# Two score buffers, two job banks: both outputs of a job share one two-bank score buffer, the freed bank becomes a seventh score bank, and single banks are released by split exponentials

## The chip, the cores and the metric

The kernel runs on one core of a Trainium2 chip. The metric is the device time of one execution in microseconds (us). The engines are named as the profile names them: PE (matmul), PEld (the weight loads that run ahead of the matmuls), DVE, ACT, POOL, and SP, which only issues transfers.

## The reference

One block of 2048 tokens with 512 features: 32 attention heads of width 16 that share one key and one value head, a gated feed-forward layer with 1376 inner features, and a per-token gate that mixes the two.

```python
g = sigmoid((x * gate_w).sum(-1, keepdims=True))
q = (x @ wq) -> 32 heads of 16;  k = x @ wk;  v = x @ wv
p = softmax(q @ k.T * 16 ** -0.5)           # per head, 2048 x 2048
a = (p @ v -> 2048 x 512) @ wo
b = (gelu_tanh(x @ w_gate) * (x @ w_up)) @ w_down
return g * a + (1 - g) * b                  # all in fp32; wq and wk are drawn 8 times larger
```

## The kernel before

After a prologue (projections of q, k, v, the first feed-forward chunk) everything is one long list of steps for PE, written out by hand as `PLAN`, 62 lines. `play` reads a line letter by letter, and PE executes the instructions in that order. The kinds of work are:

- **S (a score pair).** `scores(n, third)` makes the scores of two heads for 128 keys and 512 queries: two matmuls of 51 rows (L745), one on rows 0 to 63 and one on rows 64 to 127 of the array, which write the two banks of one score buffer of 2 x 512 fp32. Then ACT takes the exponential of all 1024 columns in one instruction (L749) into a buffer `p`. There are 1024 such pairs. `S` uses score buffers 0 and 1 in turn, `Z` uses buffer 2.
- **V (a value visit).** `pv` multiplies the exponentials of two score pairs (four heads) with the values: four products on four column strips of 32 (L816; the profile shows two matmul instructions for each, so eight for a V). They are summed over 16 V in the one bank `acc`. After the 16th, `norm` has DVE copy `acc` out (L759 or L770), and the next V needs that bank. There are 512 V.
- **F (one step of a job).** A job is a pair of long matmul chains into two banks z and y: gate and up projection of a feed-forward chunk (`gate_job`, 24 F), a part of the down projection (`down_job`), or the output projection (`wo_job`). `H` takes the banks and makes the generator `pair_mm`; each `F` issues one z matmul and one y matmul (L515), on the two row halves; `R` ends the job and has its banks evacuated. There are 61 jobs with 1608 F.
- **T** lets the GELU chain of the last gate job go on to its Tanh on ACT; the rest of the chain (`outer`, `halves`) follows two and three score pairs later.

`pair_mm` runs each chain in two halves. In the first half z is computed on the lower rows and y on the upper, in the second half the other way round. So in the middle of a job each bank passes from one row half to the other, and a no-operation on POOL (`relay`, L523) waits for the last matmuls of the first half; the first matmuls of the second half wait for it. At every third F `slot` issues a queued piece of DVE and POOL work: splitting a weight tile in two parts (`split_part`: DVE cast L186, POOL subtraction L187, then `fetch` issues the next load on SP), or a step of the softmax normalisation (`bg`).

The PSUM pools are three score buffers of two banks each (`ps_s`), one bank for `acc` (`ps_a`) and one bank (`ps_f`). While a job runs, z lies in the first bank of score buffer 2 and y in the `ps_f` bank, so that two score buffers are left; the second bank of buffer 2 lies idle. At `R` a gate job's `gelu` copies z to SBUF (L541), and runs `inner` (L544, L545); y stays in its bank until `outer` (L552), behind the Tanh.

Weight tiles arrive from DRAM in a ring of four staging buffers `st`, three loads ahead. The order on each engine is fixed when the kernel is built; at run time the engines only wait for one another.

Of the kernel before, what the change touches and what calls it, by code (L numbers as in the profile page):

```python
# [19 lines left out]
P = 128  # L20
S = 2048
# [22 lines left out]
STAGE = 4  # L44
PLAN = [
# [66 lines left out]
def mix_kernel(ctx, tc, xT, wq, wo, wf, out):  # L112
# [424 lines left out]
    def gelu(n, g, u):  # L537
        flush(chain)
        gs = cp.tile([P, TG], F32, tag="gs", name=f"gs{n}", bufs=1)
        sq = cp.tile([P, TG], F32, tag="sq", name=f"sq{n}", bufs=1)  # L540
        nc.vector.tensor_copy(gs, g)  # L541

        def inner():
            nc.vector.scalar_tensor_tensor(sq, gs, GC, gs, op0=ALU.mult, op1=ALU.mult)  # L544
            nc.vector.scalar_tensor_tensor(sq, sq, 1.0, gs, op0=ALU.add, op1=ALU.mult)  # L545

        def tanh():
            nc.scalar.activation(sq, sq, AF.Tanh, bias=0.0, scale=GS)  # L548

        def outer():  # L550
            nc.vector.scalar_tensor_tensor(sq, sq, 1.0, gs, op0=ALU.add, op1=ALU.mult)
            nc.vector.scalar_tensor_tensor(gs, u(), 0.5, sq, op0=ALU.mult, op1=ALU.mult)  # L552

        def halves():
            hh, hl = h_tiles(n)
            nc.vector.tensor_copy(hh, gs)
            nc.vector.tensor_sub(hl, gs, hh)
            hold.append((n, hh, hl))

        chain.extend((inner, tanh, outer, halves))  # L560
# [14 lines left out]
    def gate_job(n):  # L575
        tg, r = chunks[n]

        def begin():
            flush(todo)
            queue_parts(parts(n))  # L580
            return weights_terms(n, 0), weights_terms(n, 1)

        def end(z, y):
            gelu(n, z, lambda: y)
            advance(3)()
            if r == NF - 1 and tg + 1 < NTG:
                queue_parts(x_parts(tg + 1))

        return begin, end
# [134 lines left out]
    gelu(1, g1, lambda: up1)  # L724
# [4 lines left out]
    at = {}  # L729

    def scores(n, third):
# [10 lines left out]
        ps = two_banks("s", 2 if third else next(i for i in turn if i < 2))  # L742
        for j in range(2):
            rs = slice(64 * j, 64 * j + QK)
            nc.tensor.matmul(ps[:, j * TG : (j + 1) * TG], kp[rs, kc * P : (kc + 1) * P],  # L745
                             Q[u][rs, pr], start=True, stop=True)
        if pr == 0:
            pb[s] = m2.tile([P, 2, 2 * TG], F32, tag="p", name="p", bufs=PB // 2)
        nc.scalar.activation(pb[s][:, pr], ps, AF.Exp, bias=0.0, scale=SCALE)  # L749
# [72 lines left out]
    def score(third):  # L822
        scores(at_s[0], third)
# [11 lines left out]
    def play(word, job):  # L835
        if job:
            X, Y = job[0]()
        for t in word.split():
            k = int(t[1:] or 1)
            if t[0] in "SZ":  # L840
                for _ in range(k):
                    score(t[0] == "Z")
# [89 lines left out]
```

## Time and profile before

| | |
|---|---|
| median of 3 runs | 1230.35 us (1230.30 to 1230.39) |
| span of the profiled execution | 1229.5 us, mean granted clock 0.999 |
| prologue, 0 to 80.5 us | PE busy 78.29 us |
| list of steps, 80.5 to 1213.8 us | PE busy 1133.17 us, ACT busy 993.55 us, DVE 473.65 us |
| last output projection, 1213.8 to 1229.5 us | PE busy 11.12 us |
| exponentials | 1024 of 1024 columns, 976.3 us on ACT |
| score pairs / V / F in the list | 1024 / 512 / 1608 |

The profiled execution's own time is known by its span, 0.85 us under the median of the runs. Matmuls are pipelined and their ends modelled, so that PE's busy share says little; what counts is the spacing of their starts. A row of the timeline gives start, duration, engine, line, operation, output from inputs, and in brackets how long the engine stood idle before it and what the profile takes for the releaser.

### The profile page before, as it was taken

The page shows a single profiled execution, that of the slowest core. Times are in us where ns is not written, and L with a number is a line of the kernel's source. Part 1 is how long each engine was busy: PE and PEld are TensorE (multiplying, and loading weights), DVE is VectorE, ACT ScalarE, POOL GpSimd, SP SyncE. Part 2 cuts the span into 40 slices and gives each one's busy share as a digit, 9 for nine tenths or more (in the row PEclk, how much of TensorE's full clock was granted, in tenths as well). Part 3 has the DMA queues.
Part 4 walks back from the last instruction along what each step waited for, and adds up shares of the span by engine and source line. Part 5 has one row for each costly group of instructions (what it writes and reads, how often), then busy time and mean ns, then how long its engine had stood idle before and what let it go on. Part 6 is the DMA issues. An engine that isn't in the chain of part 4 may idle for free.

```text
span 1229.5 us, 23232 instructions
## 1 busy us (share of the span) xinstructions
PE 1222.6 (99%) x9742; PEld 671.4 (55%) x9742; DVE 546.1 (44%) x812; ACT 1029.4 (84%) x1127; POOL 216.9 (18%) x188
## 2 busy tenths in 40 slices
PE   9999999999999999999999999999999999999998
PEld 6875455555554555455555555654554555545545
DVE  7774422656245151545436152263626244044624
ACT  5549888888888888998888888889888898889983
POOL 5422201222121010212112020121311011012100
PEclk9999999999999999999999999999999999999999
DMA  8641202212021110122211120111211211002000
GB/s 333 211 135 52 72 1 58 66 53 79 27 68 51 44 32 23 49 57 67 66 35 58 39 76 15 42 44 56 83 41 49 75 49 32 23 27 66 15 1 35
DMA packets 39835, 73.88 MB, mean 60 GB/s; under 512 B 5488, under 2 KB 5744, under 8 KB 39728
## 3 DMA queue, kind: packets, MB, share of 16 engines
q1 hardware_dynamic: 39184, 71.32, 18.9%
q8 instruction: 77, 1.26, 0.4%
q0 software_dynamic: 256, 0.79, 0.2%
q14 instruction: 30, 0.25, 0.1%
q10 hardware_dynamic: 288, 0.26, 0.1%
HBM read 57.41 MB, written 14.94 MB: 59 GB/s over the span
## 4 chain that ended last, share of the span: by engine, by line
PE 93%; DVE 0%; ACT 0%; issue 0%
PE acc L816 38%; PE s L745 23%; PE z L515 21%; PE y L515 10%; PE wos L501 1%; PE u L501 0%; DVE acc L627 0%; ACT p L749 0%; PE wof L501 0%; DVE sq L545 0%; DVE sq L544 0%; DVE gs L541 0%; ACT sq L548 0%
## 5 line engine op out<-in xcount | busy, mean ns | idle before, releaser
L749 ACT ACTIVATE p<-s 128x1024 f32<-128x1024 f32 x1024 | 976.3, 1026 | 139.1 <-PE s L745 136.2
L816 PE MATMUL acc<-p,v 128*32 128x512 f32 x4096 | 484.8, 597 | 0.0
L745 PE MATMUL s<-Q,kp 51*128 51x512 f32 x2048 | 384.8, 415 | 0.1
L745 PEld LDWEIGHTS s<-Q,kp 51*128 51x128 f32 x2048 | 184.2, 184 | 214.1 <-ACT p L749 124.0
L816 PEld LDWEIGHTS acc<-p,v 128*32 128x32 f32 x4096 | 114.3, 109 | 250.8 <-issue 242.1
L187 POOL TENSOR_TENSOR gl<-st,gh 128x512 fp32r<-128x512 f32 x80 | 114.0, 1444 | 754.3 <-PE s L745 375.5
L515 PE MATMUL z<-xh,gh 64*128 64x512 f32 x312 | 125.9, 403 | 0.0
L515 PE MATMUL y<-xh,gh 64*128 64x512 f32 x312 | 125.8, 403 | 0.0
L515 PE MATMUL y<-xl,gh 64*128 64x512 f32 x312 | 122.4, 392 | 0.0
L515 PE MATMUL z<-xl,gh 64*128 64x512 f32 x312 | 122.1, 391 | 0.0
L515 PE MATMUL z<-xh,gl 64*128 64x512 f32 x312 | 121.8, 390 | 0.0
L515 PE MATMUL y<-xh,gl 64*128 64x512 f32 x312 | 121.7, 390 | 0.0
L541 DVE COPY gs<-z 128x512 f32<-128x512 f32 x39 | 27.0, 692 | 195.3 <-PE y L515 128.5
L187 POOL TENSOR_TENSOR dl<-st,dh 128x512 fp32r<-128x512 f32 x44 | 57.3, 1304 | 127.8 <-PE s L745 94.0
L515 PE MATMUL z<-dh,hh 64*128 64x512 f32 x176 | 69.5, 395 | 0.0
L515 PE MATMUL y<-dh,hh 64*128 64x512 f32 x176 | 69.5, 395 | 0.0
L515 PE MATMUL y<-dl,hh 64*128 64x512 f32 x176 | 68.9, 392 | 0.0
L515 PE MATMUL z<-dl,hh 64*128 64x512 f32 x176 | 68.8, 391 | 0.0
L515 PE MATMUL z<-dh,hl 64*128 64x512 f32 x176 | 68.8, 391 | 0.0
L515 PE MATMUL y<-dh,hl 64*128 64x512 f32 x176 | 68.7, 391 | 0.0
L515 PEld LDWEIGHTS z<-xh,gh 64*128 64x128 f32 x312 | 58.0, 186 | 15.6 <-POOLq L523 7.3
L515 PEld LDWEIGHTS z<-xl,gh 64*128 64x128 f32 x312 | 58.3, 187 | 8.2
(173 smaller groups left out, 1458.0 us busy)
## 6 DMA issues: line engine op xcount, KB each, us to landing
st<-wf SPq DMA_DIRECT2D x125, 256.0 KB
scr<-q SPq DMA_DIRECT2D x16, 512.0 KB
Q<-scr SPq DMA_DIRECT2D x64, 128.0 KB
Q<-scr SPq DMA_DIRECT2D x64, 64.0 KB
out<-acc SPq DMA_DIRECT2D x16, 256.0 KB
xr<-xT SPq DMA_DIRECT2D x6, 512.0 KB
st<-xT SPq DMA_DIRECT2D x12, 256.0 KB
xr<-xT SPq DMA_DIRECT2D x4, 256.0 KB
```

What stands on the lines that cost most here:

```text
L187: eng_l.tensor_sub(lo, src, hi)
L501: nc.tensor.matmul(ps, a, b, start=(first and q == 0), stop=(last and q == len(terms) - 1), skip_group_check=True)
L515: mm = nc.tensor.matmul(ps, a[rs], b[rs], start=(half == 0 and q == 0), stop=(half == 1 and q == len(X) - 1), skip_group_check=True)
L541: nc.vector.tensor_copy(gs, g)
L745: nc.tensor.matmul(ps[:, j * TG : (j + 1) * TG], kp[rs, kc * P : (kc + 1) * P], Q[u][rs, pr], start=True, stop=True)
L749: nc.scalar.activation(pb[s][:, pr], ps, AF.Exp, bias=0.0, scale=SCALE)
L816: nc.tensor.matmul(accp[u][32 * j : 32 * j + 32], vt[:, kc], pb[s][:, j // 2, (j % 2) * TG : (j % 2 + 1) * TG], start=(kc == 0), stop=(kc ...
```

## The change

- z and y are now the two banks of score buffer 2 (`z, y = bank[4:6]`). At `R` a gate job's `gelu` copies z to `gs` and at once forms `t = 0.5 * y * gs` from y; the chain then needs no PSUM: `inner` works from `gs`, its scratch tile `sq` comes from the staging ring `st`, and `outer` is one product with `t`. The number of DVE instructions is the same (seven for a chunk).
- The `ps_f` bank is a seventh score bank, `bank[6]`, for the whole list. The score buffers are allocated once, and the dependencies go by the bank written or read.
- A step for scores now names its banks: `A`, `B`, `C` are the three buffers with one exponential of 1024 columns; `a`, `b`, `c` are the same buffers with two exponentials of 512 columns; a digit `i` puts the first head in bank 6 and the second in bank `i`, with two exponentials of 512.
- The list of steps is new. It has the same 1024 score pairs, 512 V, 61 jobs and 1608 F. 448 of the score pairs have one exponential, 576 have two (283 small letters, 293 digits).

The diff, cut to its core (three of the 62 lines of the list):

```diff
+SCORES = "ABCabc012345"
 PLAN = [
-    "t: S2",
-    "f: H F7 S F3 S F2 S F3 S F3 S F3 S F3 R S V Z S T S V3 S Z S V2 S",
-    "f: H F3 S F3 S F4 S F2 S V S F3 S F3 S F3 S F3 R S V S2 T Z V3 S2 Z V3 S Z S V2 S",
-    "f: H F3 S F3 S F3 S F3 S F3 S F3 S F3 S F3 R S V S2 T Z V3 S2 Z V3 Z S2 V2 S",
...
+    "t:",
+    "f: H F 0 F4 B F3 1 F4 B 0 F6 B F3 a F3 R B 0 V4 T B",
+    "f: H F2 A F3 B F3 a F4 b 0 F5 B F5 1 F2 R b V2 A T C 2 V3 A 3",
+    "f: H F5 A F4 b F3 a 2 V2 A F2 B F4 a F3 2 F3 R A 3 V2 A T 2 c V3 A B",
...
     def gelu(n, g, u):
         flush(chain)
         gs = cp.tile([P, TG], F32, tag="gs", name=f"gs{n}", bufs=1)
-        sq = cp.tile([P, TG], F32, tag="sq", name=f"sq{n}", bufs=1)
+        t = cp.tile([P, TG], F32, tag="sq", name=f"t{n}", bufs=1)
         nc.vector.tensor_copy(gs, g)
+        nc.vector.scalar_tensor_tensor(t, u, 0.5, gs, op0=ALU.mult, op1=ALU.mult)
 
         def inner():
+            sq = cp.tile([P, TG], F32, tag="st", name="sq", bufs=STAGE)
             nc.vector.scalar_tensor_tensor(sq, gs, GC, gs, op0=ALU.mult, op1=ALU.mult)
-            nc.vector.scalar_tensor_tensor(sq, sq, 1.0, gs, op0=ALU.add, op1=ALU.mult)
+            nc.vector.scalar_tensor_tensor(gs, sq, 1.0, gs, op0=ALU.add, op1=ALU.mult)
 
         def tanh():
-            nc.scalar.activation(sq, sq, AF.Tanh, bias=0.0, scale=GS)
+            nc.scalar.activation(gs, gs, AF.Tanh, bias=0.0, scale=GS)
 
         def outer():
-            nc.vector.scalar_tensor_tensor(sq, sq, 1.0, gs, op0=ALU.add, op1=ALU.mult)
-            nc.vector.scalar_tensor_tensor(gs, u(), 0.5, sq, op0=ALU.mult, op1=ALU.mult)
+            nc.vector.scalar_tensor_tensor(t, gs, 1.0, t, op0=ALU.add, op1=ALU.mult)
...
+    pair = [ps_s.tile([P, 2 * TG], F32, tag=f"s{i}", name=f"pair{i}") for i in range(3)]
+    bank = [pair[i // 2][:, i % 2 * TG : i % 2 * TG + TG] for i in range(6)]
+    bank.append(ps_f.tile([P, TG], F32, tag="pf", name="bank6"))
 
-    def scores(n, third):
+    def scores(n, where):
...
-        ps = two_banks("s", 2 if third else next(i for i in turn if i < 2))
+        if where.isdigit():
+            two = 6, int(where)
+        else:
+            i = "abc".index(where.lower())
+            two = 2 * i, 2 * i + 1
         for j in range(2):
             rs = slice(64 * j, 64 * j + QK)
-            nc.tensor.matmul(ps[:, j * TG : (j + 1) * TG], kp[rs, kc * P : (kc + 1) * P],
-                             Q[u][rs, pr], start=True, stop=True)
+            nc.tensor.matmul(bank[two[j]], kp[rs, kc * P : (kc + 1) * P], Q[u][rs, pr], start=True, stop=True)
...
-        nc.scalar.activation(pb[s][:, pr], ps, AF.Exp, bias=0.0, scale=SCALE)
+        if where.isupper():
+            nc.scalar.activation(pb[s][:, pr], pair[i], AF.Exp, bias=0.0, scale=SCALE)
+        else:
+            for j in range(2):
+                nc.scalar.activation(pb[s][:, pr, j * TG : (j + 1) * TG], bank[two[j]], AF.Exp, bias=0.0, scale=SCALE)
...
             elif t[0] == "H":
                 advance(1)()
-                z = two_banks("z", 2)[:, 0:TG]
-                y = ps_f.tile([P, TG], F32, tag="pf", name="y")
+                z, y = bank[4:6]
                 pairs = pair_mm(z, y, X, Y)
...
-    tail = [two_banks(f"wos{h}")[:, 0:TG] for h in range(3)]
-    tail.append(ps_f.tile([P, TG], F32, tag="pf", name="wof"))
+    tail = bank[0:5:2] + bank[6:]
```

More of the change, by code (lines that the diff above doesn't have):

```diff
@@ L539, in gelu @@
         gs = cp.tile([P, TG], F32, tag="gs", name=f"gs{n}", bufs=1)
-        sq = cp.tile([P, TG], F32, tag="sq", name=f"sq{n}", bufs=1)
+        t = cp.tile([P, TG], F32, tag="sq", name=f"t{n}", bufs=1)
         nc.vector.tensor_copy(gs, g)
+        nc.vector.scalar_tensor_tensor(t, u, 0.5, gs, op0=ALU.mult, op1=ALU.mult)
         def inner():
+            sq = cp.tile([P, TG], F32, tag="st", name="sq", bufs=STAGE)
             nc.vector.scalar_tensor_tensor(sq, gs, GC, gs, op0=ALU.mult, op1=ALU.mult)
-            nc.vector.scalar_tensor_tensor(sq, sq, 1.0, gs, op0=ALU.add, op1=ALU.mult)
+            nc.vector.scalar_tensor_tensor(gs, sq, 1.0, gs, op0=ALU.add, op1=ALU.mult)
         def tanh():
-            nc.scalar.activation(sq, sq, AF.Tanh, bias=0.0, scale=GS)
+            nc.scalar.activation(gs, gs, AF.Tanh, bias=0.0, scale=GS)
         def outer():
-            nc.vector.scalar_tensor_tensor(sq, sq, 1.0, gs, op0=ALU.add, op1=ALU.mult)
-            nc.vector.scalar_tensor_tensor(gs, u(), 0.5, sq, op0=ALU.mult, op1=ALU.mult)
+            nc.vector.scalar_tensor_tensor(t, gs, 1.0, t, op0=ALU.add, op1=ALU.mult)
         def halves():
             hh, hl = h_tiles(n)
-            nc.vector.tensor_copy(hh, gs)
-            nc.vector.tensor_sub(hl, gs, hh)
+            nc.vector.tensor_copy(hh, t)
+            nc.vector.tensor_sub(hl, t, hh)
             hold.append((n, hh, hl))
@@ L583, in end @@
         def end(z, y):
-            gelu(n, z, lambda: y)
+            gelu(n, z, y)
             advance(3)()
@@ L723, in mix_kernel @@
     chain_mm(up1, weights_terms(1, 1))
-    gelu(1, g1, lambda: up1)
+    gelu(1, g1, up1)
     load_q(1)
@@ L820, in mix_kernel, with score @@
     at_s, at_v = [0], [0]
-    def score(third):
-        scores(at_s[0], third)
+    def score(where):
+        scores(at_s[0], where)
         at_s[0] = min(at_s[0] + 1, 2 * nsteps)
@@ L839, in play @@
             k = int(t[1:] or 1)
-            if t[0] in "SZ":
-                for _ in range(k):
-                    score(t[0] == "Z")
+            if t in SCORES:
+                score(t)
             elif t[0] == "V":
```

116 rows, old and new, of the table PLAN are left out of this document.

## Prediction

> **What bounds the kernel now.** I read four views: the page's chain of waits and groups, the stretch that holds the list of steps, the list of who waited for whom, and PE's timeline. The page:
>
> ```profile
> PE 93%; DVE 0%; ACT 0%; issue 0%
> ...
> L749 ACT ACTIVATE p<-s 128x1024 f32<-128x1024 f32 x1024 | 976.3, 1026 | 139.1 <-PE s L745 136.2
> ...
> L541 DVE COPY gs<-z 128x512 f32<-128x512 f32 x39 | 27.0, 692 | 195.3 <-PE y L515 128.5
> ```
>
> The chain that ended last runs on PE nearly throughout, and ACT, the other loaded engine, stood idle 139.1 us before its exponentials, nearly all of it for scores. The stretch from the first score pair to the last V, with PE, PEld, DVE, ACT and POOL in this order:
>
> ```profile
> 80.50:1213.80 1133.30, 1133.17 (x9362) 601.59 (x9361) 473.65 (x685) 993.55 (x1065) 184.05 (x134) 1.00 0.16 47
> ```
>
> So the list takes 1133.3 us and everything else of the 1229.5 us span 96.2. The question is whether PE ever stands still in those 1133.3 us. The list of waits seems to say so:
>
> ```profile
> PEld s L745 <- ACT p L749: 124.0, 160, 0.8
> ...
> PEld s L745 <- ACT sq L548: 11.7, 14, 0.8
> ...
> PEld z L515 <- POOLq L523: 8.8, 30, 0.3
> ```
>
> The first row reads like 124 us lost to ACT. But the second blames another instruction and has the same size, 11.7/14 = 0.84 us each, with the same maximum. A wait that is as long whoever is blamed is a fixed cost of the place. PE's timeline shows the place:
>
> ```profile
> 604.36 2.78 PE L816 MATMUL acc<-p,v 128*32 128x512 f32 x24
> 607.07 0.50 PE L745 MATMUL s<-Q,kp 51*128 51x512 f32 x2
> ...
> 614.60 0.39 PE L745 MATMUL s<-Q,kp 51*128 51x512 f32 x2
> 614.91 1.07 PE L816 MATMUL acc<-p,v 128*32 128x512 f32 x8
> 615.91 0.50 PE L745 MATMUL s<-Q,kp 51*128 51x512 f32 x2
> 616.25 0.39 PE L515 MATMUL y<-dh,hh 64*128 64x512 f32 x1
> ...
> 619.98 0.40 PE L745 MATMUL s<-Q,kp 51*128 51x512 f32 x2
> ```
>
> From start to start, one V (8 matmuls) takes 1.00 us to the next score pair and three take 2.71: 0.855 us for each V and 0.145 for the group. Going in costs 0.31 where a score pair is otherwise followed after 0.23 (next fence), going out 0.34 in place of 0.23. A group of V therefore costs 0.08 + 0.145 + 0.11 = 0.335 us beside its V, however long it is. The list before has 219 groups: 73 us. The other fixed loss is in the middle of a job, where a bank passes from one row half to the other over POOL:
>
> ```profile
> 140.19 0.41 PE L745 MATMUL s<-Q,kp 51*128 51x512 f32 x2
> 140.48 0.49 PE L515 MATMUL z<-xh,gh 64*128 64x512 f32 x1
> 140.48 0.49 PE L515 MATMUL y<-xh,gh 64*128 64x512 f32 x1
> 140.81 0.39 PE L515 MATMUL z<-xl,gh 64*128 64x512 f32 x1
> ```
>
> Here one score pair covers the handover: 0.29 and 0.33 us in place of 0.23 each, 0.16 lost. With two score pairs there nothing is lost, two pairs in 0.46:
>
> ```profile
> 241.92 0.65 PE L745 MATMUL s<-Q,kp 51*128 51x512 f32 x4
> 242.38 0.40 PE L515 MATMUL y<-xh,gh 64*128 64x512 f32 x1
> ```
>
> As a check of the whole: 2632 pairs (1024 score pairs, 1608 F) x 0.23 + 512 V x 0.855 + 219 x 0.335 + 30 x 0.16 = 1121 us of the 1133.3; the rest is the rounding of 0.23 and the first steps. PE is at its own spacings; there is no large wait for a seventh score bank to remove. What the change can save is groups and handovers, and what it can lose is new waits.
>
> **The change part by part.** All counts are of letters in the two lists.
>
> *Groups of V.* The new list has 206, as more V stand in runs of two and three (4 groups of one V in place of 53). 13 x 0.335 = -4.4 us. Twelve groups are followed by an F in place of a score pair; nothing shows that turn before, and I take the same 0.34 (both use row halves), bounds 0.23 to 0.44, so at most 1.3 us either way.
>
> *Middle of a job.* Before, 36 of 61 jobs have one score pair there, and 30 waits on POOL's row answer to that. The new list has two score pairs or a V in every one. 30 x 0.16 = -4.8 us; bounds 0 and 36 x 0.16 = 5.8.
>
> *Pairs, F and V themselves.* The same numbers, shapes and instructions: nothing. Score pairs wrote two banks before and do so now.
>
> *Split exponentials.* 576 score pairs get two ACT instructions of 512 columns. No exponential of 512 is in the trace; the nearest rows, start to start on ACT:
>
> ```profile
> 11.93 1.17 ACT L252 CAST kp<-gf 32x512 fp32r<-32x512 f32 x2
> ...
> 17.18 0.59 ACT L278 CAST q<-pq 128x512 fp32r<-128x512 f32 x1
> 17.67 0.63 ACT L410 ACTIVATE sqf<-sqf 96x512 f32<-96x512 f32 x1
> ...
> 82.76 2.84 ACT L749 ACTIVATE p<-s 128x1024 f32<-128x1024 f32 x3
> ...
> 620.47 1.94 ACT L749 ACTIVATE p<-s 128x1024 f32<-128x1024 f32 x2 [0.16 <-PE s L745]
> ```
>
> Three full exponentials in 2.84 us, each 1.03 long, follow each other after (2.84 - 1.03)/2 = 0.905: they overlap. A 512-column read of a score-like bank is followed after 0.49 (17.18 to 17.67); the pair at 11.93 does not overlap, 1.17/2 = 0.585. I take 0.49, as the exponentials of this kernel do overlap, and keep 0.585. ACT's work in the list is then 448 x 0.905 + 1152 x 0.49 + 40 Tanh x 0.52 (0.63 long like the one at 17.67, less the overlap of some 0.11) = 991 us, against 946 before by the same prices; the new list gives PE 1124 us. That leaves ACT 133 us idle. It is off the path and costs nothing, as long as banks come back in time.
>
> By the Trainium skill, page "ScalarE: Activation LUTs", section "What ACT_TABLE_LOAD costs", an activation with immediate scale and bias takes 186 ns and 0.833 ns a column, and neighbours overlap by about 93 ns: an estimate of 0.946 for a full and 0.52 for a half exponential. By it ACT would have 1044 us of work and 80 us idle, and the sum below would stay, with less margin. The measured 0.905 is under the page's 0.946, so I go by the rows.
>
> *Banks that come back sooner.* A score bank is wanted again after five pairs (1.16 us) at 53 places, always one released by the first half of a split. From a score pair's start to its exponential is 0.49 us (619.98 to 620.47), the first half lasts some 0.59 to 0.63, and the release takes:
>
> ```profile
> 84.74 0.19 PEld L745 LDWEIGHTS s<-Q,kp 51*128 51x128 f32 x2 [0.38 <-ACT p L749]
> ```
>
> 0.05 (the second exponential from 82.76 ends at 82.76 + 0.905 + 1.03 = 84.69). That is 1.13 to 1.17: it just fits when ACT is free. I worked the fourth line through by hand: its first `2` wants bank 2 at 3.49 us after H and gets it at 3.47; the `3` after R wants bank 6 at 9.73 and gets it at 9.76, because two splits stand right before it. So 0 to about 0.07 us late in a line, 0 to 4 us in 61 jobs. I take 0: the weight load of a score pair starts 0.2 us ahead and can come later.
>
> *Both banks evacuated at once.* DVE has the same seven instructions. The second one after R now reads y, so buffer 2 is free two passes after R in place of one:
>
> ```profile
> 609.96 0.69 DVE L759 COPY n<-acc 128x512 f32<-128x512 f32 x1 [9.21 <-PE acc L816]
> ...
> 620.88 0.75 DVE L617 SCALAR_TENSOR_TENSOR acc<-z,gc,acc 128x512 f32<-128x512 f32 x1 [9.18 <-PE z L515]
> ```
>
> The last F began at 619.98 + 0.46 = 620.44 and DVE at 620.88, so it starts about 0.2 after R: bank 4 is free at 0.95, bank 5 at 1.7. The new list uses bank 4 first after 1.32 us and a whole buffer 2 after 2.18 us at the earliest. Cover: DVE is idle when R comes (195.3 us before 39 copies, 5 us each). Tanh gets its input 0.7 us later than before; between R and T the new list mostly has two to four V, so ACT rarely waits. Cost 0, bounds 0 and 61 x 0.3.
>
> *acc.* At five places the next V comes 1.04 us after a 16th V (before: 4.29 at the earliest), and the copy takes 0.69 of it. If DVE is inside another step of 0.7 us then, PE waits. DVE is busy 42% of the stretch: 5 x 0.42 x 0.2 = +0.4 us; bounds 0 and 5 x 0.7.
>
> *Scratch in the staging ring.* Once in a chunk `sq` takes a slot of `st`, and the next loads on SP go to the slot just split, so they wait for POOL's subtraction. SP does that already, with up to 36 us at a time:
>
> ```profile
> SPq L349 <- POOL gl L187: 428.9, 62, 36.3
> ```
>
> Behind it on SP are Q loads, issued 14 V ahead (over 30 us), and output stores. Cost 0.
>
> Sum: -4.4 - 4.8 + 0.4 = -8.8 us, the profiled 1229.5 to 1220.7. The median of the runs is 0.85 above the span; 1230.35 - 8.8 = 1221.5 us.
>
> **The rivals.**
>
> *ACT becomes the bound (slower).* If half exponentials don't overlap, as at 11.93, ACT has 448 x 0.905 + 1152 x 0.585 + 21 = 1100 us of work. ACT can't fill all its idle time, because during runs of V it drains its banks; if half of the 139 us stays, 70, the list takes 1170 in place of 1124: 1268 us. It decides from (1124 - 70 - 426)/1152 = 0.545 us a half; at 0.555 the kernel is slower than before. Against it: 17.18 and 82.76. 14%.
>
> *The 0.84 us before score pairs are waits for ACT after all.* Then fewer groups save nothing by themselves, and only the handovers are left: 1226 us. For it: 160 of the waits are put down to ACT. Against: the equal 0.84 under another name. 8%.
>
> *The new fits are late.* A score pair that waits costs 0.34 in place of 0.23; at the 53 five-pair places that is 5.8 us, and with acc's 3.5 most of the gain is gone: 1230 us. For it: 0.01 to 0.03 us to spare in the line worked by hand. 12%, and 6% that delays feed each other, with splits queued behind splits, and the kernel ends some us slower, about 1238.
>
> **How the numbers follow.** The forecast has 60%, with a range of its own of 1218 (the first steps' waits gone too) to 1226. A measurement here can tell about 0.2%, 2.5 us, from no change. Faster: 60 + 8 = 68%. Same: 12, less one that falls beyond = 11%. Slower: 14 + 6 + 1 = 21%. The range from 1217 to 1240 leaves out the ACT bound and little else.
>
> **What would show it.** Right: 206 gaps of 0.84 before score pairs after V, no POOLq wait before z, the stretch near 1124 us, ACT busy about 1040 us in it, L749's halves about 0.6 long and 0.48 to 0.5 apart. Wrong: halves over 0.55 apart; waits of score pairs for ACT inside F runs; V that waits for DVE's copy of acc; ACT idle well under 100 us with PE's chain broken by ACT.

## The result, and the profile after

The changed kernel takes 1292.04 us (1291.94 to 1292.98, 5 runs) against 1230.36: ratio 1.0502 [1.049, 1.0515], 5% slower where 0.7% faster was forecast. The profiled execution has a span of 1291.2 us. The stretch of the list of steps, with PE, PEld, DVE, ACT and POOL, granted clock, DMA share and GB/s in this order:

```profile
79.50:1276.00 1196.50, 1188.91 (x9361) 619.49 (x9360) 452.19 (x687) 1027.08 (x1641) 183.54 (x134) 1.00 0.16 45
```

1196.5 us in place of 1133.3: the whole loss of 61.7 us is in the list. The page's chain of waits, and its groups of instructions (busy time, mean ns, idle time before and its releaser):

```profile
PE 85%; ACT 7%; issue 1%; DVE 0%; SPq 0%; DMA 0%; DVEq 0%; ACTq 0%
...
L758 ACT ACTIVATE p<-pair 128x1024 f32<-128x1024 f32 x448 | 449.6, 1034 | 91.3 <-PE pair L754 85.4
L761 ACT ACTIVATE p<-pair 128x512 f32<-128x512 f32 x859 | 479.3, 615 | 38.9 <-PE pair L754 36.9
...
L754 PEld LDWEIGHTS pair<-Q,kp 51*128 51x128 f32 x1755 | 194.0, 184 | 229.5 <-ACT p L761 128.9
...
L761 ACT ACTIVATE p<-bank 128x512 f32<-128x512 f32 x293 | 179.6, 613 | 26.9 <-PE pair L754 21.1
```

PE's 93% of the chain became 85%, and ACT has 7% of it. Yet ACT is not full: in the whole execution it still stands idle 91.3 + 38.9 + 26.9 = 157 us before exponentials, for scores. PE waits for ACT, and ACT waits for PE. The list of waits:

```profile
PEld pair L754 <- ACT p L761: 128.9, 263, 0.8
...
PEld pair L754 <- ACT p L758: 35.2, 87, 0.8
...
PEld bank L754 <- ACT p L761: 21.5, 48, 3.2
```

350 waits for exponentials before the weight load of a `pair` bank, where there were 160; no POOLq row stands before z any more. Sorted by their place in the list of steps, 130 of the changed kernel's waits for an exponential come right after a V; they are 0.84 us each, as before, and cost no more. New are 143 waits before the second matmul of a digit, 0.36 us each, and some 130 of about 0.23 us before score pairs that follow an F or another score pair. One place, in the timeline of ACT, PEld and PE (start, duration):

```profile
131.68 2.58 ACT L761 ACTIVATE p<-pair 128x512 f32<-128x512 f32 x5
...
132.60 0.19 PEld L754 LDWEIGHTS bank<-Q,kp 51*128 51x128 f32 x1
...
133.32 0.18 PEld L754 LDWEIGHTS pair<-Q,kp 51*128 51x128 f32 x1 [0.54 <-ACT p L761]
133.33 0.50 PE L754 MATMUL pair<-Q,kp 51*128 51x512 f32 x1
133.75 0.16 PEld L828 LDWEIGHTS acc<-p,v 128*32 128x32 f32 x8 [0.25 <-issue]
```

This is a digit, `2`: first head in bank 6 at 132.60, second head in bank 2. Bank 2 is the lower half of buffer `b`, whose two half exponentials are the second and third of the five in the first row. They are (2.58 - 0.61) / 4 = 0.49 apart and 0.61 to 0.62 long, so the one that read bank 2 ended at 132.79 and the one that read bank 3 at 133.28. The load for bank 2 came at 133.32, some 0.05 us after the exponential that read the other bank had ended. Of 293 digits, 156 hold PE by more than 0.06 us, 58 us in all by the spacing of PE's starts, and at 147 of them the load starts about 0.05 us after the end of an exponential that read the other bank of the same buffer.

### The profile page after: what moved, and what is told of

Its sections match the earlier page's. It is cut to its first block, busy times and chain, and to the rows that moved or that the text cites. A ratio compares the mean times of both kernels' runs of the same rounds, so it can differ in the third digit from the quotient of the medians.

```text
span 1291.2 us, 23747 instructions
## 1 busy us (share of the span) xinstructions
PE 1278.2 (99%) x9742; PEld 689.4 (53%) x9742; DVE 522.9 (40%) x812; ACT 1062.9 (82%) x1703; POOL 216.1 (17%) x188
## 3 DMA queue, kind: packets, MB, share of 16 engines
q1 hardware_dynamic: 39184, 71.32, 18.3%
q8 instruction: 77, 1.26, 0.4%
## 4 chain that ended last, share of the span: by engine, by line
PE 85%; ACT 7%; issue 1%; DVE 0%; SPq 0%; DMA 0%; DVEq 0%; ACTq 0%
PE acc L828 35%; PE pair L516 25%; PE pair L754 20%; PE bank L754 5%; ACT p L758 3%; ACT p L761 3%; PE pair L502 1%; DMA Q<-shs 0%; PE bank L502 0%; DVE acc L629 0%; SPq L369 0%; SPq L374 0%; SPq L368 0%; DVE ol L806 0%; DVE n L771 0%
## 5 line engine op out<-in xcount | busy, mean ns | idle before, releaser
L758 ACT ACTIVATE p<-pair 128x1024 f32<-128x1024 f32 x448 | 449.6, 1034 | 91.3 <-PE pair L754 85.4
L761 ACT ACTIVATE p<-pair 128x512 f32<-128x512 f32 x859 | 479.3, 615 | 38.9 <-PE pair L754 36.9
L754 PE MATMUL pair<-Q,kp 51*128 51x512 f32 x1755 | 425.2, 429 | 3.9 <-ACT p L761 2.0
L754 PEld LDWEIGHTS pair<-Q,kp 51*128 51x128 f32 x1755 | 194.0, 184 | 229.5 <-ACT p L761 128.9
L761 ACT ACTIVATE p<-bank 128x512 f32<-128x512 f32 x293 | 179.6, 613 | 26.9 <-PE pair L754 21.1
L516 PE MATMUL pair<-xh,gh 64*128 64x512 f32 x624 | 145.2, 399 | 0.0
L516 PE MATMUL pair<-xh,gl 64*128 64x512 f32 x624 | 144.5, 395 | 0.0
L516 PE MATMUL pair<-xl,gh 64*128 64x512 f32 x624 | 144.0, 393 | 0.0
L754 PE MATMUL bank<-Q,kp 51*128 51x512 f32 x293 | 119.9, 409 | 2.8 <-ACT p L761 2.8
L516 PE MATMUL pair<-dh,hl 64*128 64x512 f32 x352 | 76.3, 392 | 0.0
```

Of the source, the lines that this page charges most:

```text
L516: mm = nc.tensor.matmul(ps, a[rs], b[rs], start=(half == 0 and q == 0), stop=(half == 1 and q == len(X) - 1), skip_group_check=True)
L754: nc.tensor.matmul(bank[two[j]], kp[rs, kc * P : (kc + 1) * P], Q[u][rs, pr], start=True, stop=True)
L758: nc.scalar.activation(pb[s][:, pr], pair[i], AF.Exp, bias=0.0, scale=SCALE)
L761: nc.scalar.activation(pb[s][:, pr, j * TG : (j + 1) * TG], bank[two[j]], AF.Exp, bias=0.0, scale=SCALE)
```

## The experiments

The kernel before took 1230.36 to 1230.46 us (medians) beside each group of runs.

| kernel | median us | ratio to before [95%] |
|---|---|---|
| changed kernel | 1292.04 | 1.0502 [1.049, 1.0515] |
| e1_own_bank: changed, second matmul freed from the other bank's reader | 1234.75 | 1.0035 [1.0022, 1.0047] |
| e2_before_split: before, 576 exponentials split | 1232.75 | 1.0017 [1.0007, 1.0026] |
| e3_small_whole: changed, small letters not split | 1285.23 | 1.0442 [1.0425, 1.046] |
| e4_old_list: changed, with the old list | 1247.08 | 1.0133 [1.0116, 1.015] |
| e5_start: e1 with another start | 1231.42 | 1.0008 [0.9999, 1.0017] |
| e6_few_splits: e5, 65 of 283 small letters split | 1231.97 | 1.0013 [1.0004, 1.0022] |
| e7_short: e5, exponentials a quarter shorter | 1221.05 | 0.992 [0.9907, 0.9934] |
| e8_before_short: before, exponentials a quarter shorter | 1229.44 | 0.9991 [0.9982, 1.0] |
| e9_retuned: e5, list retuned | 1231.84 | 1.001 [1.0001, 1.0019] |
| e10_retuned_mid: e9, middle of jobs kept covered | 1228.36 | 0.9983 [0.9974, 0.9992] |

### e1_own_bank

Theory A: a bank is released with its buffer, not by itself. The edit keeps the changed list and every instruction, and drops only the order between a score matmul and exponentials that read the other bank of the buffer it writes into:

```diff
             mm = nc.tensor.matmul(bank[two[j]], kp[rs, kc * P : (kc + 1) * P], Q[u][rs, pr], start=True, stop=True)
+            own_bank(mm, two[j])   # for each name in reads[other bank]: tc.declare_no_dep(mm.ins, name)
...
-                nc.scalar.activation(pb[s][:, pr, j * TG : (j + 1) * TG], bank[two[j]], AF.Exp, ...)
+                e = nc.scalar.activation(pb[s][:, pr, j * TG : (j + 1) * TG], bank[two[j]], AF.Exp, ...)
+                reads[two[j]].append(e.ins.name)
```

> The changed kernel, with one thing different: a score matmul no longer waits for the exponential that reads the other bank of its two-bank buffer (the dependency is dropped; the exponential that read its own bank is still waited for). Theory A (in the changed kernel a bank is released with its whole buffer, so a digit's second matmul is held by some 0.4 us until the other bank has been read, 147 times, and more for small letters): most of the 75 us that PE loses in the list comes back, 1222 to 1237 us. Theory B (the 576 split exponentials overload ACT): ACT's work is the same, 1280 us or more. Theory C (evacuating both job banks at once, or the quick reuse of acc, holds PE): 1280 us or more.

Measured 1234.75 us: 57.3 of the 61.7 us are gone. The same digit in its timeline:

```profile
128.22 1.60 ACT L769 ACTIVATE p<-pair 128x512 f32<-128x512 f32 x3
...
129.18 0.19 PEld L761 LDWEIGHTS bank<-Q,kp 51*128 51x128 f32 x1
129.38 0.18 PEld L761 LDWEIGHTS pair<-Q,kp 51*128 51x128 f32 x1
...
129.42 0.46 PE L761 MATMUL pair<-Q,kp 51*128 51x512 f32 x1
...
129.81 0.16 PEld L837 LDWEIGHTS acc<-p,v 128*32 128x32 f32 x8 [0.24 <-issue]
```

The halves are 0.48 apart; the first of `b`, the second in the row, ends at 128.70 + 0.64 = 129.34, and the load follows at 129.38, while the other half (the third in the row) runs until 129.82. From bank 6's load to V's it is 0.63 us in place of 1.15. The idle time before the loads for `pair` banks falls from 229.5 us by 53:

```profile
L761 PEld LDWEIGHTS pair<-Q,kp 51*128 51x128 f32 x1755 | 190.1, 184 | 176.1 <-ACT p L769 86.8 <-ACT p L766 35.3 <-issue 25.1
```

The order between the engines was kept by the framework (the program that turns the kernel's Python into instructions and waits) for the tile, and the tile is the two-bank buffer. The chip did not ask for it. The Trainium skill says the same (page "PSUM — Partial Sum Buffer", section "PSUM bank collisions raise a hardware error"): two engines may not be in the same bank and quadrant at once, and guarding by bank is enough. The trace agrees: here the matmul into bank 2 begins at 129.42, while ACT is still reading bank 3 of the same buffer.

### e2_before_split and e3_small_whole

Theory B: the splits themselves cost ACT so much that banks come late. e2 splits 576 of the 1024 exponentials of the kernel before; e3 takes the split out of the small letters of the changed kernel.

```diff
+        if (n + 1) * 9 // 16 == n * 9 // 16:
             nc.scalar.activation(pb[s][:, pr], ps, AF.Exp, bias=0.0, scale=SCALE)
+        else:
+            for j in range(2):   # one exponential for each bank
```

> The kernel before, with 576 of its 1024 exponentials (evenly spread) split into two of 512 columns; list, banks and jobs as before. It has the ACT work of the changed kernel and none of its bank sharing. Theory A: a buffer comes back about 0.07 us later and ACT has some 35 us more work in 139 us of idle time: 1232 to 1245 us. Theory B: most of the loss, 1270 us or more. Theory C: no change, 1230 to 1235 us.

```diff
-        if where.isupper():
+        if not where.isdigit():
```

> The changed kernel, with the small letters a, b, c read by one exponential of 1024 columns like A, B, C; only the 293 digits are split. Theory A: with the release by whole buffers a split of a, b, c frees nothing early and ends 0.07 us later, so taking it away gains a little: 1278 to 1290 us. Theory B: half of the additional ACT work is gone, about 1260 us. If banks were released one by one in the changed kernel, the digits behind a small letter would now wait 0.4 us each, 1300 us or more.

e2: 1232.75 us, 2.3 more than the 1230.46 beside it; 576 splits cost about 4 ns each where banks are not wanted early. That lies in the ranges of both A and C; Theory B falls. e3: 1285.23 us, 6.8 less than the changed kernel. When both banks are released together anyway, one exponential of 1.03 us gives them back sooner than two halves that end 0.49 + 0.61 = 1.10 us after the first began: in the changed kernel the small letters' splits did the opposite of what they were there for.

### e4_old_list

Old list in the new code: z and y in buffer 2, both evacuated at once, no digit and no split (`Z` became `C`, `S` became `A` and `B` in turn).

> The changed kernel with the list of before (S as A and B in turn, Z as C): z and y in the two banks of buffer 2, both evacuated at once, no split exponential, bank 6 left idle. Theory A: only the score pairs that take buffer 2 within 1.7 us after R wait, 23 of them some 0.45 us and 18 some 0.15: 1238 to 1248 us. Theory B: not slower than before by more than that. Theory C (the evacuation holds PE): 1270 us or more.

1247.08 us, 16.6 more than the 1230.46 beside it. The waits name the places:

```profile
PEld pair L754 <- DVE t L543: 20.7, 27, 1.3
```

27 score pairs after `R` want buffer 2 before DVE has read y out of it. The row is not the loss: 14 of these pairs stand behind a V and wait some 1.26 us, of which 0.84 are PE's own; the other 13 follow a score pair and wait 0.24. Nor are all 16.6 us due to the evacuation, since e4 has the stall at the start too that the next run is about:

```profile
PE pair L754 <- ACT p L758: 2.3, 1, 2.3
```

With that taken off at the 3.3 us that e5 gives for it, some 13 us are left, which is also what the expectation's 23 x 0.45 + 18 x 0.15 come to. The bound of this step in the prediction, 61 x 0.3 = 18.3 us, holds for a list that doesn't make room. The new list does, and no wait for that line is among the larger ones of the changed kernel.

### e5_start

e1 still loses time at one place, 82 us after the start, where PE stands 2.5 us. The changed kernel shows the same place in its waits from 81 to 85 us and in the windows around it:

```profile
ACT gs L551 <- DVE gs L548: 8.8, 1, 8.8
...
PEld bank L754 <- ACT p L761: 3.2, 1, 3.2
...
DVE sq L547 <- POOL dl L188: 1.5, 1, 1.5
```

```profile
79.00:82.00 3.00, 3.00 (x23) 2.07 (x21) 1.02 (x2) 0.00 (x0) 1.24 (x1) 1.00 0.48 128
82.00:85.00 3.00, 0.21 (x3) 0.10 (x1) 2.12 (x4) 1.37 (x3) 0.06 (x1) 0.84 0.33 102
85.00:89.00 4.00, 4.00 (x18) 3.23 (x20) 3.70 (x4) 2.89 (x5) 2.77 (x2) 0.50 0.37 125
89.00:95.00 6.00, 5.79 (x43) 4.08 (x43) 2.25 (x5) 5.03 (x10) 0.00 (x0) 0.84 0.02 4
```

`inner` of the first gate job takes its scratch from the staging ring and waits 1.5 us until POOL has read that slot; the Tanh behind it stands first in ACT's queue, and the first exponentials behind the Tanh. PE then stands 2.8 us for a bank, and its granted clock is 0.50 in the next 4 us. The edit does two things, which this run doesn't take apart: it issues that chain before the part that uses the slot, and moves the first score pairs away from it:

```diff
-    "t:",
-    "f: H F 0 F4 B F3 1 F4 B 0 F6 B F3 a F3 R B 0 V4 T B",
+    "t: 0 B",
+    "f: H F8 1 F4 B 0 F6 B F3 a F3 R B 0 V4 T B",
...
-    split_part(("d", 2, 0))
     chain.pop(0)()
+    split_part(("d", 2, 0))
```

> The kernel with the own-bank release, and a mended start: the first two score pairs (0, B) stand ahead of the first job, and the first chunk's inner comes before the split of the d tile, so that its scratch tile does not wait for POOL's subtraction in that staging slot. Theory D (at the start DVE waited 1.5 us for the slot, the Tanh behind it stood ahead of the first exponentials in ACT's queue, PE stood 2.8 us and its granted clock then fell to 0.60 for some microseconds): the first steps give back 4 to 6 us, 1229 to 1231 us. Rival: the start is hidden by what follows, 1234 to 1235 us.

1231.42 us, 3.3 less than e1, somewhat less than expected. The clock stays at 1.00; of the stall, one wait for POOL at the first handover is left:

```profile
PEld pair L516 <- POOLq L524: 0.7, 1, 0.7
```

### e6_few_splits

e5 is at the time of before, though groups and handovers are saved. Is ACT's backlog after runs of V what makes the rest late (theory E), or the time that a single exponential takes (rival F)? Only the 65 small letters whose lower bank is wanted within 1.8 us by a digit stay split.

> The same, and of the 283 small letters only 65 are still split: those whose first bank is taken next by a digit soon after. The others have one exponential of 1024 columns, so ACT has 218 instructions and some 13 us of work less, and those buffers come back 0.07 us sooner. Theory E (what is left over the forecast is score pairs that wait about 0.1 us for a bank at some hundred places, because splits queue behind splits on ACT): 1222 to 1227 us, which beats the kernel before. Rival F (those waits come from the fixed times from score pair to exponential and from the list, not from ACT's work): within 1 us of the kernel with the mended start.

1231.97 us, within 0.6 of e5. So the small letters' splits are not what makes the rest late. Theory E as a whole does not fall with it, since the 586 halves of the digits stayed. e5's trace says how much is ACT's queue: at 160 score pairs that don't follow a V, the load starts 0.05 us after the end of the exponential that last read its bank. At 97 of them that exponential had begun within 0.62 us of its own scores, so only the fixed times are left; at 63 it had begun later, nearly always behind other work of ACT. 83 of the 160 wait for a whole exponential.

### e7_short and e8_before_short

If it is the time of exponentials, a bank's own or those ahead of it on ACT, shortening each must free it. Every exponential covers three quarters of its columns; V's second read of a pair starts at column 256, so PE's instructions stay the same.

```diff
-nc.scalar.activation(pb[s][:, pr], pair[i], AF.Exp, ...)
+nc.scalar.activation(pb[s][:, pr, 0 : 2 * CUT], pair[i][:, 0 : 2 * CUT], AF.Exp, ...)   # CUT = 384
...
-... pb[s][:, j // 2, (j % 2) * TG : (j % 2 + 1) * TG]
+... pb[s][:, j // 2, (j % 2) * (2 * CUT - TG) : (j % 2) * (2 * CUT - TG) + TG]
```

> The kernel with released banks and the mended start (1231.4 us), with every exponential over 384 columns of a bank in place of 512 (768 in place of 1024 for a whole one); V's second read of a pair starts 256 columns into it, so that PE's instructions keep their number and shapes. The last quarter of the scores is left out. Theory T: about 10 us of that kernel are score pairs that wait some 0.1 us for the exponential of their own bank, five pairs (1.16 us) after it for a half and seven (1.63 us) for a whole one. A half gets shorter by about 0.1 us and a whole one by about 0.2, so nearly all of it goes: 1220 to 1224 us, about what groups of V and handovers were to bring. Rival U: what is left over the floor is PE's own spacing and the list simply isn't shorter: 1230 to 1232.

> The kernel before, with the same shortening of its exponentials (768 of 1024 columns). If 0.84 us before each score pair after V was PE's own and nothing there waits for ACT, as both T and the forecast have it: 1228.5 to 1231 (no change beyond 2 us). If those were waits for ACT (the second rival of the prediction): some 160 waits shorter by up to 0.2 us, 1200 to 1220.

e7: 1221.05 us, 10.4 under e5. e8: 1229.44 us, 1.0 under before. Their stretches of the list, after that of e5 without the shortening:

```profile
79.79:1214.47 1134.68, 1133.22 (x9361) 609.91 (x9361) 452.85 (x687) 1021.71 (x1641) 183.84 (x134) 1.00 0.16 47
```

```profile
79.50:1204.20 1124.70, 1123.25 (x9362) 604.89 (x9362) 452.76 (x687) 837.51 (x1641) 183.53 (x134) 1.00 0.17 48
```

```profile
80.50:1211.80 1131.30, 1130.95 (x9354) 596.44 (x9351) 472.41 (x686) 814.80 (x1065) 182.46 (x133) 1.00 0.16 47
```

So some 9 us of e5 were score pairs that waited for their own bank: of the 160 late loads e7 has 3 left. How much of that is the time of the bank's own exponential and how much ACT's queue, e7 can't tell, because it makes both shorter. In e1's timeline such waits look like this, one behind a whole exponential that began at 134.14, one behind the half that began at 135.06 in bank 6:

```profile
134.14 1.03 ACT L766 ACTIVATE p<-pair 128x1024 f32<-128x1024 f32 x1
135.06 0.59 ACT L769 ACTIVATE p<-bank 128x512 f32<-128x512 f32 x1
```

```profile
135.22 0.19 PEld L761 LDWEIGHTS pair<-Q,kp 51*128 51x128 f32 x2 [0.22 <-ACT p L766]
...
135.71 0.18 PEld L761 LDWEIGHTS bank<-Q,kp 51*128 51x128 f32 x1 [0.18 <-ACT p L769]
```

Both loads start 0.05 us after the exponential ended, too late to be hidden; both exponentials had begun some 0.5 us after their scores. e8 also settles the second rival. Before, 160 waits of score pairs were put down to ACT, 124.0 us in all; with exponentials 0.2 us shorter the time moves by 1 us, and what is put down to ACT is still 0.83 us each:

```profile
PEld s L746 <- ACT p L750: 110.2, 133, 0.8
```

They were PE's own.

### e9_retuned and e10_retuned_mid

Can the list make that room? Score pairs inside runs of F move by one to three F, or change their letter, so that a half finds its bank again after six or seven pairs in place of five, a whole one after eight in place of seven, by the intervals measured above. Two lines of e10:

```diff
-    "f: H F2 A F3 B F3 a F4 b 0 F5 B F5 1 F2 R b V2 A T C 2 V3 A 3",
-    "f: H F5 A F4 b F3 a 2 V2 A F2 B F4 a F3 2 F3 R A 3 V2 A T 2 c V3 A B",
+    "f: H A F5 B F3 a F4 B 0 F6 B F6 1 R b V2 A T C 2 V3 A 3",
+    "f: H F6 A F3 b F3 a 2 V2 A B F5 A F3 2 F4 R A 3 V2 A T 2 c V3 a B",
```

> The kernel with released banks and the mended start, its exponentials whole, with a list in which score pairs inside runs of F are moved by one to three F, or their letter is changed, so that a bank is wanted again later: half five pairs after its use becomes six or seven, whole seven becomes eight, where there is room. V, F, R, T and the groups of V stay where they are. Theory T: most of the 10 us goes, at fixed ACT work: 1222 to 1227, faster than the kernel before by 0.3 to 0.7%. Rival U: 1230 to 1232.

1231.84 us: nothing gained, against Theory T's expectation. One row of its waits tells why:

```profile
PEld pair L516 <- POOLq L524: 10.5, 26, 0.8
```

The moves had taken score pairs out of the middle of 27 jobs, where they cover the handover over POOL. e10 is the same retuning with two score pairs or a V kept there.

> The list retuned as in the run before (1231.8 us), but with two score pairs or a V kept in the middle of every job. In that run, 27 jobs had lost this: 7 to 9 had no score pair there, 15 one, and its trace shows 20 places of about 0.17 us where F waits after a score pair, 3.4 us in all, beside some 8 us of banks that come back late. Theory T with the handover at its price: 1224 to 1228 us, 0.2 to 0.5% faster than the kernel before. Rival U (moving score pairs wins nothing, since what one place gains another loses): 1229 to 1232.

1228.36 us, between the two expectations, and 2 such waits left of 26:

```profile
PEld pair L516 <- POOLq L524: 1.6, 2, 0.8
```

Covering those middles again is worth 3.5 us. The rest of the retuning is worth about 3 us (e5 to e10), a third of what e7 showed to be there. That runs of F have not enough F for all is my reading; no run shows it. e10 is the only version that computes everything and is faster than both kernels, by 0.17% [0.08, 0.26] against the one before, which is about the limit of what can be told.

## Why the prediction was wrong

The step that failed is **"Banks that come back sooner"**, by its premise: that a bank wanted again after five pairs is "released by the first half of a split". With it failed the sentence on the change that the dependencies go by the bank written or read. The release goes by the buffer, the two-bank tile. I worked the fits through for banks, found 0.01 to 0.03 us to spare, and never asked what the wait was attached to. The trace of before couldn't show it, since every exponential there covered both banks of its buffer; a bound for "both banks are released by the second half" would have been one half's period, 0.49 us, at the 293 digits, 144 us at most, and would have stood among the rivals. Dropping the false order gave back 57.3 us (e1).

From the forecast 1221.5 to the measured 1292.04 are 70.5 us. The edits, one on top of the other, gave back 57.3 (release by buffer, e1), 3.3 (the start, e5) and 10.4 (shorter exponentials, e7), of which 1.0 is what the kernel before gains by the same shortening (e8): 70.0 in all.

- **Groups and middles of jobs**, -4.4 and -4.8: right in sum. With short exponentials on both sides the new list is 1229.44 - 1221.05 = 8.4 us shorter. Each by itself is not shown; e9 to e10, 3.5 us for 27 middles, 7 to 9 of them without any score pair, is of the size of the second.
- **Split exponentials**, 0, halves every 0.49: right on the interval (0.48 to 0.49), and 2.3 us on the cost (e2). The 946 us of ACT work before should read 947.5 by the same prices, which changes nothing. By the Trainium skill, page "ScalarE: Activation LUTs", it would be 0.52; the rows were nearer, as for the full one. ACT, the first rival at 14%, never became the bound: in e5 it is busy 1021.71 of the list's 1134.68 us.
- **Fits that are late**, the third rival at 12 and 6%: right in kind once banks are released by themselves, and close in size by luck. It measured 10.4 us less the 1.0 that before also gains; the rival gave 9.3, of which 3.5 were acc, and the other 5.8 were 0.11 at each of 53 places five pairs apart. The loss came at 160 places, about 0.06 us each; only some 25 are five pairs apart, and 83 wait for whole exponentials, which I hadn't priced. It was no rival but part of the sum: from a score pair to its exponential 0.5 to 0.6, a half 0.615, the release 0.05, against 1.16 us. I took 0 because a weight load that starts 0.2 ahead can come later. This alone would have made the forecast "no change" (e5).
- **Both banks evacuated at once**, 0: right, by the room that the list leaves; without it some 13 us (e4 less the start).
- **Scratch in the staging ring**, 0: wrong at one place, the first gate job. I looked at what queues behind SP, not at DVE's own wait for POOL's read of the slot with ACT's queue behind it: 2.8 us of standing and a slow clock after it, 3.3 us by e5.
- **acc**, +0.4: about right. The trace after has 0.9 us of PE idle for DVE's copy, at one place.
- **The 0.84 us are waits for ACT**, 8%: falls. They are still 0.83 us each with exponentials 0.2 us shorter (e8).

## What to carry to other kernels

Before counting on a part of a buffer being released early, find out what the wait hangs on: here the order between engines was kept for the allocated tile, and a split of the reader alone makes the release later (1.10 us in place of 1.03). An instruction that waits for another engine and starts 0.05 us after the end of one that read other data is the sign of it. And where a buffer comes back after a fixed time, set that time against the distance to its next use at every place, not only at the nearest ones: margins of 0.01 to 0.03 us, found by hand in one line, became some 9 us over 160 places.

## What the runs showed of the hardware

- PE's granted clock fell to half after it had stood 2.8 us in the changed kernel and 2.5 us in e1. In the first it was 0.50 from 84.04 on, when PE still stood, for 6.8 us; in the second from 85.78 on, 0.85 us after PE had gone on, for 3.4 us (the two rows below). The Trainium skill, page "TensorE: Matmul & The Clock Gate", Part 1, gives half rate after an idle window of about 3.4 us that runs freely; the traces show half rate, after gaps somewhat shorter than that window.

```profile
84.04:90.86 6.82, 5.96 (x27) 4.97 (x29) 4.79 (x7) 5.28 (x10) 2.77 (x2) 0.50 0.33 111
```

```profile
85.78:89.19 3.41, 3.41 (x20) 2.42 (x18) 3.21 (x4) 3.41 (x7) 2.44 (x2) 0.50 0.39 103
```

- The 0.05 us from the end of an exponential to the weight load that waits for it came out the same within 0.01 us for whole exponentials, for halves, for the own bank and for the other bank.
